# A chunked RWKV-7 recurrence with a squared-ReLU FFN on one core: products written in turn to two partition halves, x made by halves, sums and words taken earlier

## The chip, the cores and the metric

The kernel runs on one core of a Trainium2 chip. Its engines each work through their own list of instructions in order: TensorE (PE in the profile; PEld is its weight load) multiplies matrices and writes PSUM, VectorE (DVE) and ScalarE (ACT) read PSUM and work elementwise, GpSimd (POOL) works elementwise on SBUF, SyncE (SP) issues DMAs. ACT and POOL issue DMAs too. The metric is the device time of one execution in microseconds (us), lower is better.

## The reference

Four sequences, 8 heads, 768 steps, head size 40. Each head keeps a 40 x 40 state; then a feed-forward layer of width 2048 works on the result.

```python
for t in range(S):
    y[:, :, t] = np.einsum('bhd,bhde->bhe', rt, state)
    Sa = np.einsum('bhde,bhe->bhd', state, at)
    state_decay = state * wt[:, :, None, :] - np.einsum('bhd,bhe->bhde', Sa, bt)
    state = state_decay + np.einsum('bhd,bhe->bhde', vt, kt)
...
x = attn_out.transpose(0, 2, 1, 3).reshape(B * S, H * D)      # 3072 x 320
h = np.maximum(x @ w_in, 0.0)
return h * h @ w_out
```

All inputs and outputs are float32 for the chip's program.

## The kernel before

The 768 steps are cut into 6 chunks of 128, which gives 24 chunks (sequence by sequence within a chunk number), and `order` counts them 0 to 23. Within a chunk the recurrence becomes matrix products. Let a, b, k, r be scaled by running decays (`up`, `down`). Then

- `early` makes, for each head, the products of b and a (`products`), from which come N, the coupling of the chunk's first 64 rows to its last 64, and two triangular 64 x 64 blocks whose inverses are needed. Five ACT copies take them from PSUM into the tile `N` (lines 399 to 403); DMAs carry them to DRAM: `kept_q` or `kept_d` for the blocks, `kept_m` and `kept_n` for the rest.
- The triangular blocks are inverted on POOL by substitution (`solving`, lines 469 to 489), many heads and chunks side by side. A *unit* is what POOL inverts at once: 1 to 4 chunks. Units 0 to 8 invert quarter blocks of 32; units 9 and 10, chunks 16 to 19 and 20 to 23, invert blocks of 64 in 63 steps. `take` fetches a unit's words into `half_n`, `solving` stores the result in `kept_t`, and `inverses` loads it from there as T for one chunk.
- `chain` does what only follows from the state. x = a·state + A·v, for 128 rows, is gathered in one PSUM bank (`x_`). Its first half is copied by ACT into `x_first`, multiplied by T (here T0), copied back, multiplied by N and added to the second half of x in the bank; the second half is copied to `x_second` and multiplied by T (here T1). The result, negated, is `minus_x`. Heads go in pairs: 4 products of 128 x 64 by 128 x 80 each for T0, N and T1. In the trace each float32 product is two PE instructions.
- `closing` ends a chunk: the state grows by k·v and b·minus_x (both products go into one bank, `grown`; the last chunk of a sequence has none), and the outputs `y_` gather RV·k and RX·b. RV and RX are masked products. ACT copies the last decay into `end`.
- `Ffn` works on pairs of chunks (*groups*, 0 to 11): `thirds` and `whole` are x·w_in, ReLU and square are on ACT (lines 777 and 784), and `make_quarter` is the product with w_out. From group 5 on, that product is done by seven block products for eight (Strassen's way), the *pieces* P1 to P7 (`make_piece`), whose sums DVE makes. In groups 5 to 10, P6, P5 and P3 write three parts of one PSUM bank. For the last group each has a bank of its own.

Up to chunk 7 the order of the work is a list of words written by hand (the *opening*; `f` is a product of the identity, `fill_in`, whose result nobody reads: the word's number is 128-column blocks). From chunk 7 on a fixed order repeats, one *slot* per chunk (`sorted_slot`): a slot does the end of its chunk's chain, prepares the next chunk, makes in slots 7 to 13 one or two early parts of later chunks, and does FFN work between. At its end stand the squares, then the next chunk's x (slots 7 to 22, 16 of them), and then the steps of `closing` alternate with T0, N and T1 of the next chunk's chain. Two pieces come at the end of each slot and two at the start of the next. After slot 23 follows the tail, with FFN work alone.

[...] The framework sets the semaphores between engines.

Of the kernel before, what the change touches and what calls it, by code (L numbers as in the profile page):

```python
# [17 lines left out]
def kernel(  # L18
# [341 lines left out]
    def early(i, g=None, apart=False):  # L360
# [36 lines left out]

        even, odd = products(bT, aT[:, :, :C])
        nc.scalar.copy(t_[:HC, :, :NP], even[:HC].rearrange("s h (f t) -> s f h t", f=2))  # L399
        nc.scalar.copy(t_[HC:, 1, NP:], even[HC:, :, HC:])  # L400
        nc.scalar.copy(t_[HC:, 1, :NP], odd[:HC, :, :HC])
        nc.scalar.copy(t_[:HC, 0, NP:], odd[HC:, :, HC:])
        nc.scalar.copy(t_[:HC, 1, NP:], odd[:HC, :, HC:])
        moved = []
# [13 lines left out]
        if g is None:  # L418
            moved.append((kept_n[i].rearrange("b s q t -> s b q t"), t_[:HC, 1].rearrange("s (b q) t -> s b q t", b=2), nc.sync))
        if opened:  # L420
# [207 lines left out]
    halves = (slice(0, HC), slice(HC, C))  # L628
    by_parity = lambda t_: t_.rearrange("t (q e) d -> t e q d", e=2)

    x_first, x_second = (single(name, [128, NP, 2, D]) for name in ("x_first", "x_second"))
    for t_ in (x_first, x_second):
        nc.gpsimd.memset(t_, 0.0)

    def chain(i, g):
        bb, c = order[i]
        st = states.tiles[bb]
        first, second_ = halves
        k_, b_, v_, rT = (g[x] for x in ("k", "b", "v", "rT"))

        x_ = psum(ps_c)[:, :DM].rearrange("t (h d) -> t h d", h=H)
        if c > 0:
            for q in range(NP):
                for f in range(2):
                    mm(x_[halves[f], 2 * q:2 * q + 2], g["aT"][:, q, f * HC:(f + 1) * HC], st[:, q, :, :D], q == 0)
        for h in range(H):
            for f in range(2):
                mm(x_[halves[f], h], g["A"][h % 2][:, h // 2, f * HC:(f + 1) * HC], v_[:, h, :D], c == 0 and h == 0)
        for e in range(2):
            nc.scalar.copy(x_first[halves[e], :, e], by_parity(x_)[first, e])  # L650
# [12 lines left out]
        for e in range(2):
            nc.scalar.copy(x_first[halves[e], :, e], xs[:, :, e])  # L664
        nc.scalar.copy(xn[first, :, :D], xs.rearrange("t q e d -> t (q e) d"))
        yield
        for q in range(NP):
            mm(x_[second_, 2 * q:2 * q + 2], N[:, q], both(x_first[:, q]), False)
        for e in range(2):
            nc.scalar.copy(x_second[halves[1 - e], :, e], by_parity(x_)[second_, e])  # L670
# [21 lines left out]
    def closing(i, g, y_, rx, xn):  # L692
# [46 lines left out]
    class Ffn:  # L739
# [72 lines left out]
        def make_piece(self, g, at):  # L812
# [43 lines left out]
            if at == 4:  # L856
                self.sixth = ps[0]
            if at == (4 if last else 6):
                plus(hi1, self.sixth, hi1)
                plus(hi0, self.sixth, hi0)  # L860
                less(lo1, hi1, lo1)
            if at == 5:
                self.fifth = ps[1]
            if at == (5 if last else 6):
                plus(hi1, self.fifth, hi1)
                plus(hi0, self.fifth, hi0)
            if at == 6:
                plus(hi0, ps[2], hi0)
            for n in {5: (1,), 6: (0,)}.get(at, ()) if last else (1, 0) if at == 6 else ():
# [216 lines left out]
    def sorted_slot(i, g, ch):  # L1086
# [76 lines left out]
    for i in range(LAID, len(order)):  # L1163
# [44 lines left out]
```

## Time and profile before

| | |
|---|---|
| three runs | 950.64, 959.54, 959.63 us (median 959.54) |
| the profiled execution | 953.11 us, of which the span from first to last instruction is 951.4 |
| busy | PE 885.5 us, POOL 458.3, DVE 446.3, ACT 344.7 |
| T, N and T1 instructions | 192 each (24 chunks x 4 products x 2) |
| opening, slots 7 to 22, rest | to about 330 us, to about 859 us, to 951 us |

In the rows of the timeline the first number is the start in us from the span's start, the second the length of a row of like instructions. What stands in brackets is idle time of the engine before it and what ended it. A row such as `128*64 128x80` has 128 rows of contraction, 64 output rows, and 80 columns that are streamed.

### The profile page before, as it was taken

The numbers are of one execution on the slowest core, as the hardware profiler recorded it, in microseconds if no ns is written. First come the engines' busy times: TensorE is split into PE (matmuls) and PEld (weight loads), VectorE is DVE, ScalarE is ACT, GpSimd is POOL, SyncE is SP. The second block draws the span as 40 slices with busy tenths as digits, with TensorE's granted clock in tenths as the row PEclk, the third lists the DMA queues.
The fourth block names the chain that finished last, engine by engine and source line by source line (L and its number), as shares of the span: only waits on it lengthen the run. The fifth ranks groups of instructions, "written<-read, shape, count | busy, mean of one in ns | idle before, by whom it ended". The sixth has DMA issues, their size and how long they took to land.

```text
span 951.4 us, 22372 instructions
## 1 busy us (share of the span) xinstructions
PE 885.5 (93%) x9004; PEld 741.0 (78%) x9004; DVE 446.3 (47%) x1127; ACT 344.7 (36%) x797; POOL 458.3 (48%) x869
## 2 busy tenths in 40 slices
PE   6668978879899999989999999999999999999998
PEld 5446656758687877868888878898988988888897
DVE  4827757886843343454432553363534523233022
ACT  3032334534633335524434424423333233332311
POOL 4557447083007686770189998599997000000000
PEclk9768989589899999999999999999999999999999
DMA  9759869947766578697874545544414444130000
GB/s 110 125 125 154 185 125 189 223 101 141 166 104 150 96 136 171 136 159 128 162 142 91 104 70 102 142 73 86 79 29 110 75 83 78 23 63 2 21 14 14
DMA packets 257137, 102.04 MB, mean 107 GB/s; under 512 B 235211, under 2 KB 246859, under 8 KB 256011
## 3 DMA queue, kind: packets, MB, share of 16 engines
q1 hardware_dynamic: 248613, 83.00, 48.7%
q0 software_dynamic: 3664, 15.79, 6.7%
q10 hardware_dynamic: 4757, 1.83, 0.9%
q8 instruction: 71, 1.16, 0.6%
q14 instruction: 32, 0.25, 0.1%
HBM read 67.82 MB, written 30.79 MB: 104 GB/s over the span
## 4 chain that ended last, share of the span: by engine, by line
PE 75%; DVE 8%; ACT 6%; DMA 5%; SPq 3%; issue 2%; ACTq 0%; POOL 0%; DVEq 0%; POOLq 0%
PE ps_f L87 37%; PE ps_w L87 18%; PE ps_c L87 10%; PE ps_w L331 5%; DMA in_ab<-in_b_dram 2%; PE ps_f L264 2%; DMA dec<-kept_e 1%; ACT x_first L664 1%; PE ps_c L600 1%; PE ps_c L676 1%; DMA in_r<-in_r_dram 1%; ACT hid L784 1%; DVE half_t L480 1%; DVE half_t L482 1%; SPq L421 1%
## 5 line engine op out<-in xcount | busy, mean ns | idle before, releaser
L480 POOL TENSOR_TENSOR half_p<-half_n,half_t 128x126 f32<-128x126 f32 (+43 forms) x374 | 196.4, 525 | 68.8 <-DMA half_n<-kept_q 24.2
L482 POOL TENSOR_TENSOR half_t<-half_t,half_p 128x126 f32<-128x126 f32 (+43 forms) x374 | 212.9, 569 | 29.3
L87 PE MATMUL ps_f<-tokens,w_in 128*128 128x256 f32 x672 | 157.9, 389 | 0.0
L87 PE MATMUL ps_f<-w_out,hid 128*128 128x160 f32 (+1 forms) x736 | 151.8, 359 | 0.0
L87 PEld LDWEIGHTS ps_f<-tokens,w_in 128*128 128x128 f32 x672 | 126.6, 193 | 24.2 <-issue 7.3
L87 PEld LDWEIGHTS ps_f<-w_out,hid 128*128 128x128 f32 x736 | 116.1, 190 | 22.3
L777 ACT ACTIVATE hid<-ps_f 128x512 f32<-128x512 f32 x84 | 49.2, 596 | 121.2 <-PE ps_f L87 120.4
L453 POOL DMA_DIRECT2D half_n<-kept_q x20 | 10.4, 526 | 94.7 <-DMA kept_m<-N 33.2
L708 DVE TENSOR_TENSOR state<-ps_w,state 40x160 f32<-40x160 f32 x40 | 12.8, 320 | 90.4 <-PE ps_w L87 90.1
L784 ACT ACTIVATE hid<-hid 128x512 f32<-128x512 f32 x96 | 54.6, 625 | 0.1
L347 DVE TENSOR_TENSOR RX<-ps_w,upper 128x512 f32<-128x512 f32 x48 | 30.9, 684 | 46.6 <-PE ps_w L87 46.6
L372 DVE TENSOR_TENSOR_SCAN decay<-ps_w,ones 128x64 f32<-128x64 f32 x88 | 23.8, 270 | 60.4 <-PE ps_w L331 60.4
L87 PE MATMUL ps_f<-tokens,w_third 64*128 64x256 f32 x336 | 49.9, 391 | 2.3 <-DVE o L843 2.2
L722 DVE TENSOR_TENSOR tokens<-ps_c,dec 128x512 f32<-128x512 f32 x24 | 16.6, 692 | 71.3 <-PE ps_c L87 69.9
L399 ACT COPY N<-ps_w 64x512 f32<-64x512 f32 x24 | 13.9, 579 | 99.6 <-PE ps_w L87 71.6
L264 PE MATMUL ps_f<-ident 128*128 128x512 f32 (+3 forms) x108 | 49.5, 592 | 0.0
L347 DVE TENSOR_TENSOR RV<-ps_w,upper 128x512 f32<-128x512 f32 x48 | 30.9, 685 | 18.5 <-PE ps_w L87 18.2
L87 PEld LDWEIGHTS ps_f<-tokens,w_third 64*128 64x128 f32 x336 | 31.9, 189 | 8.2 <-DVE o L843 3.8
L331 PE MATMUL ps_w<-ident,in_ab 128*128 128x128 f32 x184 | 27.6, 295 | 11.0 <-DVE RV L347 8.7
L550 DVE TENSOR_TENSOR kvT<-ps_w,dec 128x512 f32<-128x512 f32 x24 | 16.5, 686 | 43.8 <-PE ps_w L331 37.8
L87 PE MATMUL ps_w<-rT,kvT 40*128 40x128 f32 x384 | 29.5, 295 | 6.1 <-ACT kvT L563 6.1
L562 ACT COPY rT<-ps_w 128x512 f32<-128x512 f32 x24 | 14.0, 584 | 57.7 <-PE ps_w L331 57.7
(179 smaller groups left out, 1639.7 us busy)
## 6 DMA issues: line engine op xcount, KB each, us to landing
dec<-kept_e SPq DMA_DIRECT2D x22, 633.8 KB
kept_e<-decay SPq DMA_DIRECT2D x19, 633.8 KB
in_w<-in_w_dram SPq DMA_DIRECT2D x24, 160.0 KB
in_b<-in_b_dram SPq DMA_DIRECT2D x24, 160.0 KB
in_ab<-in_a_dram SPq DMA_DIRECT2D x24, 160.0 KB
in_r<-in_r_dram SPq DMA_DIRECT2D x24, 160.0 KB
in_v<-in_v_dram SPq DMA_DIRECT2D x24, 160.0 KB
half_n<-kept_q POOLq DMA_DIRECT2D x14, 256.0 KB, 4.8
```

Of the source, the lines that this page charges most:

```text
L87: nc.tensor.matmul(o, l_, r_, start=start, stop=True, skip_group_check=True)
L264: nc.tensor.matmul(fill_bank[:, :n * 128], ident, ident.unsqueeze(1).to_broadcast([128, n, 128]), start=True, stop=True, skip_group_check= ...
L331: nc.tensor.transpose(p_[:, q * 128:(q + 1) * 128], pair(x_, q), ident)
L347: nc.vector.tensor_tensor(t_, p_, over4(upper), Alu.mult)
L372: nc.vector.tensor_tensor_scan(up[:, q, MID + 1:C + 1], wT[:, q, MID:], ones, 1.0, Alu.mult, Alu.mult)
L480: eng.tensor_tensor(p_, part[:, at:at + m_].unsqueeze(1).to_broadcast([128, n, m_]), t3[:, :n, s:s + 1].to_broadcast([128, n, m_]), Alu.mult)
L482: eng.tensor_tensor(t3[:, :n, s + 1:], t3[:, :n, s + 1:], p_, Alu.subtract)
L550: nc.vector.tensor_tensor(kT, kT_, down[:, :, 1:C + 1], Alu.mult)
L562: nc.scalar.copy(g["rT"], p_)
L722: nc.vector.tensor_tensor(t_, y_, g["up"][:, :, :C], Alu.mult)
L777: nc.scalar.activation(h_, p_.rearrange("p f t -> p (f t)"), Act.Relu)
L784: nc.scalar.activation(h_, h_, Act.Square)
```

## The change

1. `chain`: T0, N and T1 take the head pairs in the order 0, 2, 1, 3, and write pairs 0 and 1 to partitions 0 to 63, pairs 2 and 3 to 64 to 127. For this the places of the heads in N and T differ: `early` fills `N` by ten ACT copies, eight of 64 x 128 and two of 64 x 256, where it took one of 64 x 512 and four of 64 x 256. `kept_n` is stored by two DMAs with runs of 512 B, where it was one with runs of 1 KB.
2. x is made by halves of its rows: `begin_x(0)`, two copies, `begin_x(1)`. One tile `apart_x` serves for `x_first` and `x_second`. The copies into `minus_x` are two of 64 x 160 for one of 64 x 320, and those of the first half come after N.
3. In the slot the chain's step comes first in each round (T0 ahead of the growth of the state), and the first of four RX products of `closing` moves ahead of T1.
4. `make_piece`: the sums with P6 and P5 follow these pieces in every group, where groups 5 to 10 made them after P3.
5. Unit 9 is inverted up to step 48, then the first 2048 words of unit 10 are fetched, then the rest of unit 9 is done.

```diff
-        even, odd = products(bT, aT[:, :, :C])
-        nc.scalar.copy(t_[:HC, :, :NP], even[:HC].rearrange("s h (f t) -> s f h t", f=2))
-        nc.scalar.copy(t_[HC:, 1, NP:], even[HC:, :, HC:])
-        nc.scalar.copy(t_[HC:, 1, :NP], odd[:HC, :, :HC])
-        nc.scalar.copy(t_[:HC, 0, NP:], odd[HC:, :, HC:])
-        nc.scalar.copy(t_[:HC, 1, NP:], odd[:HC, :, HC:])
+        for e, p_ in enumerate(products(bT, aT[:, :, :C])):
+            for group in range(2):
+                own_, qs = slice(group * HC, (group + 1) * HC), slice(2 * group, 2 * group + 2)
+                nc.scalar.copy(t_[own_, group, e:NP:2], p_[:HC, qs, :HC])
+                nc.scalar.copy(t_[own_, group, NP + e::2], p_[HC:, qs, HC:])
+            nc.scalar.copy(t_[:HC, 1, e::2], p_[:HC, :, HC:])
...
+            for e in range(2):
+                moved.append((kept_n[i][e].rearrange("s (w j) t -> s w (j t)", w=2), between[:, :, e].rearrange("s w j t -> s w (j t)"), nc.sync))
...
+    in_turn_ = (0, 2, 1, 3)
...
+        def begin_x(f):
+            cols = slice(f * HC, (f + 1) * HC)
+            if c > 0:
+                for q in in_turn_:
+                    mm(x_[halves[q // 2], f, 2 * q % NP:2 * q % NP + 2], g["aT"][:, q, cols], st[:, q, :, :D], f == 0 and q % 2 == 0)
+            for h in range(NP):
+                for e in range(2):
+                    mm(x_[halves[e], f, h], g["A"][h % 2][:, 2 * e + h // 2, cols], v_[:, e * NP + h, :D], c == 0 and f == 0 and h == 0)
...
+        begin_x(0)
+        to_apart(lambda e: x_[halves[e], 0])
+        begin_x(1)
...
-        def times_t(half, x):
-            xs = psum(ps_w)[:, :DM].rearrange("t (q c) -> t q c", q=NP)
-            for q in range(NP):
-                mm(xs[halves[half], q], T[:, half * NP + q], both(x[:, q]), q == 0)
+        def times_t(half):
+            xs = psum(ps_w)[:, :DM // 2].rearrange("t (j c) -> t j c", j=2)
+            for q in in_turn_:
+                mm(xs[halves[q // 2], q % 2], T[:, half * NP + q], both(q), q % 2 == 0)
...
+        for n in in_turn_:
+            mm(x_[halves[n // 2], 1].rearrange("t (b j) d -> t b j d", b=2)[:, :, n % 2], N[:, n], both(n), False)
+        to_xn(0, xs)
+        to_apart(lambda e: x_[halves[e], 1])
...
+        to_y(rx, b_, 0)
+        yield
+        for q in range(1, NP):
             to_y(rx, b_, q)
...
-            if at == (4 if last else 6):
+            if at == 4:
                 plus(hi1, self.sixth, hi1)
                 plus(hi0, self.sixth, hi0)
                 less(lo1, hi1, lo1)
...
-            if at == (5 if last else 6):
+            if at == 5:
                 plus(hi1, self.fifth, hi1)
                 plus(hi0, self.fifth, hi0)
...
             for _ in range(3):
+                next(n["chain"])
                 next(close)
-                next(n["chain"])
...
-            take(unit, own)
-            solve(unit)
+            words = [slice(None)] if under_way is None else [slice(0, EARLIER), slice(EARLIER, None)]
+            take(unit, own, words[0])
+            if under_way is not None:
+                run(under_way)
+                take(unit, own, words[1])
+            under_way = solving(unit, (48,) if FINE <= unit < len(units) - 1 else ())
+            next(under_way, None)
```

What it does to PE's list at the end of slot 14, where chunk 15's x stands (`state_137,dec_131` and `in_v_112,A` are x's two parts, `in_v_114` and `minus_x_132` the growth of chunk 14's state). Before:

```order
L87 MATMUL ps_c<-state_137,dec_131 64x80 [waits Activation_49]
L87 MATMUL ps_c<-state_137,dec_131 64x80 x7
...
L87 MATMUL ps_c<-in_v_112,A 64x40 x13
L87 MATMUL ps_w<-in_v_114,in_k_106 40x40 x8
L87 MATMUL ps_w<-minus_x_132,in_b_86 40x40 x8
L87 MATMUL ps_c<-RV,in_k_106 64x128 x2
L87 MATMUL ps_w<-x_first,T 64x80 [waits Activation_49]
...
L87 MATMUL ps_c<-RV,in_k_106 64x128 x6
L87 MATMUL ps_c<-x_first,N_7059 64x80 [waits DMAHW6_49,Activation_49]
...
L87 MATMUL ps_c<-RX,in_b_86 64x128 x8
L87 MATMUL ps_w<-x_second,T 64x80 [waits Activation_49]
```

And with the change, the same place:

```order
L87 MATMUL ps_c<-in_v_112,A 64x40 x5
L87 MATMUL ps_c<-state_137,dec_131 64x80 [waits Activation_49]
...
L87 MATMUL ps_c<-in_v_112,A 64x40 x8
L87 MATMUL ps_w<-apart_x,T 64x80 x4
L87 MATMUL ps_w<-in_v_114,in_k_106 40x40 x8
L87 MATMUL ps_w<-minus_x_132,in_b_86 40x40 x8
L87 MATMUL ps_c<-RV,in_k_106 64x128 x2
L87 MATMUL ps_c<-apart_x,N_7183 64x2x40 [waits DMAHW3_49,Activation_49]
...
L87 MATMUL ps_c<-RV,in_k_106 64x128 x6
L87 MATMUL ps_c<-RX,in_b_86 64x128 x2
L87 MATMUL ps_w<-apart_x,T 64x80 [waits Activation_49]
...
L87 MATMUL ps_c<-RX,in_b_86 64x128 x6
```

x stands in two parts, and the second begins with a wait for ACT; T0 has none of its own, and the growth of the state comes behind it. (The list counts a float32 product once, the trace twice.)

The second place is on PE at the end of slot 19, where P6 (`decay_127,hid`) and P5 of group 7 stand, and at the start of slot 20, where P3 stands behind the transposes of r and v. Before:

```order
L87 MATMUL ps_f<-decay_127,hid 128x160 [waits PE_49]
L87 MATMUL ps_f<-decay_127,hid 128x160 x7
L87 MATMUL ps_f<-w_out,hid 128x160 x8
L331 MATMUL ps_w<-ident,in_r_110 128x128 [waits DMAHW3_49]
...
L87 MATMUL ps_f<-w_out,hid 128x160 x8
```

And with the change:

```order
L87 MATMUL ps_f<-decay_127,hid 128x160 [waits PE_49]
L87 MATMUL ps_f<-decay_127,hid 128x160 x7
L87 MATMUL ps_f<-w_out,hid 128x160 [waits DVE_49]
L87 MATMUL ps_f<-w_out,hid 128x160 x7
L331 MATMUL ps_w<-ident,in_r_110 128x128 [waits DMAHW0_49]
...
L87 MATMUL ps_f<-w_out,hid 128x160 [waits DVE_49]
```

P5's first product waits for DVE, where it waited for nothing, and so does P3's.

The third place is on POOL, between unit 9 and unit 10 (`half_t` and `half_p` are the substitution's steps, `kept_t_233` unit 9's result). Before:

```order
L482 TENSOR_TENSOR half_t<-half_t,half_p 128x32 [waits Pool_49]
L489 DMA kept_t_233<-half_t 128x2048 [waits Pool_49]
L453 DMA half_n<-kept_d_223 64x3072 [waits DMAHW4_49,DMAHW5_49,DMAHW3_49,DMAHW6_49,DMAHW2_49,DMAHW7_49,DMAHW1_49,DMAHW0_49]
L453 DMA half_n<-kept_d_223 64x3072
L469 MEMSET half_t 128x2048 [waits DMASW1_49]
```

And with the change:

```order
L485 TENSOR_TENSOR half_t<-half_t,half_p 128x24x16 [waits Pool_49]
L456 DMA half_n<-kept_d_223 64x2048 [waits DMAHW3_49,DMAHW5_49,DMAHW2_49,DMAHW7_49,DMAHW1_49,DMAHW0_49]
L456 DMA half_n<-kept_d_223 64x2048
L483 TENSOR_TENSOR half_p<-half_n,half_t 128x375 [waits Pool_49]
...
L492 DMA kept_t_233<-half_t 128x2048 [waits Pool_49]
L456 DMA half_n<-kept_d_223 64x1024 [waits DMAHW4_49,DMAHW3_49,DMAHW6_49,DMAHW2_49,DMAHW0_49]
```

The fetch of the first words, with its wait for the stores of chunks 20 to 23, moved from behind unit 9's result to ahead of its last 15 steps.

More of the change, by code (lines that the diff above doesn't have):

```diff
@@ L418, in early @@
         if g is None:
-            moved.append((kept_n[i].rearrange("b s q t -> s b q t"), t_[:HC, 1].rearrange("s (b q) t -> s b q t", b=2), nc.sync))
+            between = t_[:HC, 1].rearrange("s (w b j) t -> s w b j t", w=2, b=2)
+            for e in range(2):
+                moved.append((kept_n[i][e].rearrange("s (w j) t -> s w (j t)", w=2), between[:, :, e].rearrange("s w j t -> s w (j t)"), nc.sync))
         if opened:
@@ L427, in early @@
             for e in range(2):
-                nc.scalar.copy(g["N"][e * HC:(e + 1) * HC], t_[:HC, 1, e * NP:(e + 1) * NP])
+                nc.scalar.copy(g["N"][e * HC:(e + 1) * HC].rearrange("s (w j) t -> s w j t", w=2),
+                               t_[:HC, 1].rearrange("s (w b j) t -> s w b j t", w=2, b=2)[:, :, e])
             g["joins"] = spare("joins", i)
@@ L628 @@
     halves = (slice(0, HC), slice(HC, C))
[L629 to L633, printed above, removed]
+    apart_x = single("apart_x", [128, NP, 2, D])
+    nc.gpsimd.memset(apart_x, 0.0)
+    in_turn_ = (0, 2, 1, 3)
     def chain(i, g):
@@ L637, in chain, with to_apart @@
         st = states.tiles[bb]
-        first, second_ = halves
         k_, b_, v_, rT = (g[x] for x in ("k", "b", "v", "rT"))
-        x_ = psum(ps_c)[:, :DM].rearrange("t (h d) -> t h d", h=H)
-        if c > 0:
-            for q in range(NP):
[L644 to L650, printed above, removed]
+        x_ = psum(ps_c)[:, :DM].rearrange("t (f h d) -> t f h d", f=2, d=D)
+        def begin_x(f):
[6 more added lines that the diff above has]
+                    mm(x_[halves[e], f, h], g["A"][h % 2][:, 2 * e + h // 2, cols], v_[:, e * NP + h, :D], c == 0 and f == 0 and h == 0)
+        def to_apart(of):
+            for e in range(2):
+                nc.scalar.copy(apart_x[halves[e], :, e], of(e))
+        begin_x(0)
+        to_apart(lambda e: x_[halves[e], 0])
+        begin_x(1)
         yield
@@ L653, in chain, with to_xn @@
         xn = minus_x.next()
-        both = lambda t_: t_.rearrange("p e d -> p (e d)")
-        def times_t(half, x):
-            xs = psum(ps_w)[:, :DM].rearrange("t (q c) -> t q c", q=NP)
-            for q in range(NP):
-                mm(xs[halves[half], q], T[:, half * NP + q], both(x[:, q]), q == 0)
-            return xs[halves[half]].rearrange("t q (e d) -> t q e d", e=2)
-        xs = times_t(0, x_first)
+        both = lambda q: apart_x[:, q].rearrange("p e d -> p (e d)")
+        def times_t(half):
+            xs = psum(ps_w)[:, :DM // 2].rearrange("t (j c) -> t j c", j=2)
+            for q in in_turn_:
+                mm(xs[halves[q // 2], q % 2], T[:, half * NP + q], both(q), q % 2 == 0)
+            return xs.rearrange("t j (w d) -> t w j d", w=2)
+        def to_xn(half, xs):
+            for e in range(2):
+                to = xn[halves[half], :, :D].rearrange("t (w b j) d -> t w b j d", w=2, b=2)[:, :, e]
+                nc.scalar.copy(to, xs[halves[e]])
+        xs = times_t(0)
         for e in range(2):
-            nc.scalar.copy(x_first[halves[e], :, e], xs[:, :, e])
-        nc.scalar.copy(xn[first, :, :D], xs.rearrange("t q e d -> t (q e) d"))
+            nc.scalar.copy(apart_x[halves[e], :, e].rearrange("t (w j) d -> t w j d", w=2), xs[halves[e]])
         yield
[L667 to L670, printed above, removed]
+        for n in in_turn_:
+            mm(x_[halves[n // 2], 1].rearrange("t (b j) d -> t b j d", b=2)[:, :, n % 2], N[:, n], both(n), False)
+        to_xn(0, xs)
+        to_apart(lambda e: x_[halves[e], 1])
         yield
-        nc.scalar.copy(xn[second_, :, :D], times_t(1, x_second).rearrange("t q e d -> t (q e) d"))
+        to_xn(1, times_t(1))
         yield
@@ L714, in closing @@
             to_y(g["RV"], k_, q)
+        to_y(rx, b_, 0)
         yield
-        for q in range(NP):
+        for q in range(1, NP):
             to_y(rx, b_, q)
@@ L868, in make_piece @@
                 plus(hi0, ps[2], hi0)
-            for n in {5: (1,), 6: (0,)}.get(at, ()) if last else (1, 0) if at == 6 else ():
+            for n in {5: (1,), 6: (0,)}.get(at, ()):
                 bb, c = order[g * GB + n]
@@ L1059 @@
     done = set(range(14))
-    unit = len(solves)
+    unit, under_way = len(solves), None
     def fetch_next(i, *names):
@@ L1171 @@
             flush()
-            take(unit, own)
-            solve(unit)
+            words = [slice(None)] if under_way is None else [slice(0, EARLIER), slice(EARLIER, None)]
[5 more added lines that the diff above has]
+            next(under_way, None)
+            if unit < FINE or unit == len(units) - 1:
+                run(under_way)
+                under_way = None
             unit += 1
```

## The prediction

> **What bounds the kernel now.** I read the page first: how much of the span each engine works.
>
> ```profile
> span 951.4 us, 22372 instructions
> PE 885.5 (93%) x9004; PEld 741.0 (78%) x9004; DVE 446.3 (47%) x1127; ACT 344.7 (36%) x797; POOL 458.3 (48%) x869
> ```
>
> TensorE (PE) is busy 93% of the span, the next engine 48%. The view by stretches says where it is not busy (columns: stretch, its length, then each engine's busy us and instructions, the clock, the DMA share).
>
> ```profile
> 618.00:648.50 30.50, 30.42 (x330) 27.75 (x329) 15.61 (x22) 9.91 (x23) 28.30 (x29) 1.00 0.33 58
> 648.50:678.40 29.90, 29.01 (x314) 25.94 (x313) 10.44 (x22) 9.46 (x21) 27.94 (x26) 1.00 0.41 74
> ```
>
> A slot (one chunk of the steady part) leaves PE 0.08 us idle of 30.5; the next leaves 0.89. A "busy" PE is not yet a PE that could do nothing else: a matmul's row holds its latency. So I looked at the end of a slot in the timeline of PE and ACT, where the changed products stand (start, length, engine, line, tiles, shape, count).
>
> ```profile
> 611.96 0.78 PE L87 MATMUL ps_c<-state,dec 128*64 128x80 f32 x16
> 612.56 1.08 PE L87 MATMUL ps_c<-in_v,A 128*64 128x40 f32 x32
> 613.47 0.48 PE L87 MATMUL ps_w<-in_v,in_k 128*40 128x40 f32 x16
> 614.08 0.42 PE L87 MATMUL ps_c<-RV,in_k 128*64 128x128 f32 x4
> 614.34 0.70 PE L87 MATMUL ps_w<-x_first,T 128*64 128x80 f32 x7
> 615.84 0.56 PE L87 MATMUL ps_c<-x_first,N 128*64 128x80 f32 x5
> 616.45 1.04 PE L87 MATMUL ps_c<-RX,in_b 128*64 128x128 f32 x14
> 617.32 0.74 PE L87 MATMUL ps_w<-x_second,T 128*64 128x80 f32 x8
> 617.99 0.81 PE L87 MATMUL ps_f<-in_ab,hid 128*128 128x160 f32 x4
> ...
> 612.56 1.14 ACT L784 ACTIVATE hid<-hid 128x512 f32<-128x512 f32 x2
> 613.69 0.59 ACT L650 COPY x_first<-ps_c 64x160 f32<-64x160 f32 x2
> 614.31 0.20 ACT L710 COPY end<-dec 128x4 f32<-128x4 f32 x1
> 615.20 0.59 ACT L664 COPY x_first<-ps_w 64x160 f32<-64x160 f32 x2 [0.69 <-PE ps_w L87]
> 616.65 0.59 ACT L670 COPY x_second<-ps_c 64x160 f32<-64x160 f32 x2 [0.41 <-PE ps_c L87]
> ```
>
> The stretch of 6.03 us (611.96 to 617.99) is a relay: x on PE, copies on ACT, T0 on PE, copies, N, copies, T1. Each hand-over takes 0.05 to 0.06 us: T0 starts 0.06 after L650's copies end (614.28), N 0.05 after L664's (615.79). PE's other rows only fill the gaps. And the copies of x start when two things end together: x (612.56+1.08 = 613.64) and ACT's squares, L784 (612.56+1.14 = 613.70).
>
> **The products in turn: what they save.** Start to start, T1's 8 instructions take 617.99-617.32 = 0.67. The state products have the same shape (128x64, 80 columns), but write to the two halves in turn: 16 in 612.56-611.96 = 0.60, or 8 in 0.30. T, N and T1 now do so too: 0.37 less each. I take 0.30; if their order gains nothing it is 0.67. Were PE's issue the bound, that were 3 x 0.37 = 1.1 per chunk.
>
> **x by halves: a wait that the text of the diff doesn't show.** The new order is first half of x, its copies, second half, T0; the second half is to run while ACT copies the first. In the list of PE's instructions its first one waits for ACT, and T0, which reads what ACT copied, waits for ACT no more. So the second half waits for those very copies: it writes the bank that they read. Queued behind the waiting instruction on PE are the rest of the slot's end and the next slot; nothing else can be issued. [...]
>
> With the rows' numbers, us from 611.96. Half of x is (613.47-611.96)/2 = 0.76, its result 0.17 later: 0.93. The copies can't start before ACT's squares end: 1.74, to 2.33. Second half 2.38 to 3.14. T0 to 3.44, result 3.61. Copies 3.66 to 4.25. PE meanwhile: the state's growth (614.08-613.47 = 0.61) and the first RV (0.26), to 4.31. N to 4.61. ACT has the end copy (0.20) and the pair of minus_x copies that now stands ahead, 0.59, so N's copies run 5.04 to 5.63. PE's other 12 RV (614.34-614.08 = 0.26 per four) and first 4 RX ((617.32-616.45)/14 = 0.062 each) last from 4.61 to about 5.6. T1 5.68 to 5.98, and 12 RX after it, 0.75: 6.73, against 6.03 now. That is +0.70. In the last three slots, which have no growth and no end copy, the same sum gives +0.60. In the first three, ACT's squares end earlier, as in this row of one of them:
>
> ```profile
> 401.16 0.59 ACT L650 COPY x_first<-ps_c 64x160 f32<-64x160 f32 x2 [0.28 <-PE ps_c L87]
> ```
>
> ACT idles 0.28 before the copies, so +0.4. Sixteen slots begin a chain (10 x 0.70 + 3 x 0.60 + 3 x 0.4 = 10.0; I take 9.6, 0.6 each, for copies that overlap by some hundredths). Ends: were there no wait, T0 would start at 2.38 as now, the same steps would end the relay at 5.93, and sixteen times -0.1 is -1.6; it is +24 if the new order of T, N and T1 gains nothing (1.5 each).
>
> **Sums of a piece.** Now six sums follow the last piece of a group, and PE waits for its bank:
>
> ```profile
> 650.76 2.34 PE L87 MATMUL ps_f<-w_out,hid 128*128 128x160 f32 x16
> 656.19 0.33 DVE L843 TENSOR_TENSOR in_w<-ps_f,in_w 128x160 f32<-128x160 f32 x1 [7.47 <-PE ps_f L87]
> 656.43 0.32 DVE L843 TENSOR_TENSOR o<-ps_f,o 128x160 f32<-128x160 f32 x1
> 658.47 1.13 PE L87 MATMUL ps_f<-tokens,w_third 64*128 64x256 f32 x6 [0.80 <-DVE o L843]
> PE ps_f L87 <- DVE o L843: 2.2, 4, 0.8
> ```
>
> The last row (the view of waits) says 2.2 us in four waits. These go: one sum of 0.32 is left after the last piece, and products of 1.1 us stand before the bank is wanted. But P5 writes the bank that P6's sums read, and its first matmul, free now, waits for DVE in the new list: 0.04 to start, two sums to 656.75 (0.56), 0.06 to PE: 0.67. P5 of group 5 is the row at 650.76; ahead of it is P6, and nothing between. Four groups in slots, two in the tail, and P3 behind P5 in the last of these: 7 x 0.67 = 4.7. Net +2.5 (-2.2 to +4.7).
>
> **The opening: copies of N, stores, and x.** N takes ten copies for five:
>
> ```profile
> L399 ACT COPY N<-ps_w 64x512 f32<-64x512 f32 x24 | 13.9, 579 | 99.6 <-PE ps_w L87 71.6 <-issue 18.6 <-DMA in_ab<-in_b_dram 6.5
> L650 ACT COPY x_first<-ps_c 64x160 f32<-64x160 f32 x48 | 13.7, 285 | 28.0 <-PE ps_c L87 27.5
> L402 ACT COPY N<-ps_w 64x256 f32<-64x256 f32 x24 | 8.9, 369 | 0.3
> ```
>
> 0.58 + 4 x 0.37 = 2.05 becomes 2 x 0.37 + 8 of 64x128. Between 64x160 (0.285) and 64x512 (0.579) an element costs 0.83 ns, so 64x128 is 0.26: 2.82, +0.78 a chunk. In a slot ACT idles past that (9.9 busy of 30.5). The opening makes N for 14 chunks; I take four of these as lying on its path (an estimate, between none and all): +3. The store of N for later chunks becomes two, one issue more on SP or ACT per chunk (0.69 in the row below), for two of them: +1.4. Then the wait of x, which is worst where ACT is behind:
>
> ```profile
> 120.36 1.13 PE L87 MATMUL ps_c<-in_v,A 128*64 128x40 f32 x32
> 121.42 6.71 PE L264 MATMUL ps_f<-ident 128*128 128x512 f32 x16
> 134.46 1.06 PE L87 MATMUL ps_w<-spares 32*32 32x32 f32 x32 [3.31 <-DVE spares L522]
> ...
> 125.64 0.69 ACTq L421 DMA_DIRECT2D kept_n<-N x1
> 127.62 0.56 ACT L650 COPY x_first<-ps_c 64x160 f32<-64x160 f32 x2
> ```
>
> x of chunk 2 ends at 121.5, its copies only at 128.2, because ACT has N's copies and seven issues first. PE fills that time with 16 fill products. With the change PE stands until 128.2+1.4 = 129.6, then the other half 0.6, the fill 6.7, and transposes and fill to 134.46 that took 6.5 but 3.3 of idle: spares at 140.1 instead of 134.46, up to +5.7. What DMA and VectorE are late by anyway swallows some: I take half, +3. Against it, T, N and T1 of eight chains, 24 x 0.37 = 8.9 at most; on the path about half, -4. Opening: +3.4, from -6 to +11.
>
> **Hidden.** Unit 10's words come early, in the midst of unit 9's solve on POOL.
>
> ```profile
> 577.27 1.84 SPq L110 DMA_DIRECT2D kept_d<-N x4
> 594.95 0.60 POOL L489 DMA_DIRECT2D kept_t<-half_t x1 [0.30 <-POOL half_t L482]
> 608.94 0.29 POOL L480 TENSOR_TENSOR half_p<-half_n,half_t 128x63 f32<-128x63 f32 x1 [6.49 <-DMA half_n<-kept_d]
> 625.66 1.83 SPq L509 DMA_DIRECT2D T<-kept_t x2
> 733.45 0.60 POOL L489 DMA_DIRECT2D kept_t<-half_t x1 [0.30 <-POOL half_t L482]
> 746.79 1.39 SPq L509 DMA_DIRECT2D T<-kept_t x2
> ```
>
> POOL would wait for the words' store (issued 577 to 579) with fifteen steps of unit 9 queued behind; unit 9's result moves from 595 to about 608, before its reader at 625.7, and unit 10's from 733 to about 740, before 746.8. Cover: 13 us, then 7. Cost none; gone, each us late is one lost.
>
> **Sum.** The profiled execution took 953.11 (span 951.4 and 1.7 around it). 953.1 + 9.6 + 2.5 + 3.4 = 968.6. The three runs' median, 959.54, lies 6.4 above it, so I add half of that: **972**.
>
> **Rivals.** *Faster: PE's issue is the bound.* If the second half of x starts before ACT's squares end (the point that decides) and PE finds work for every gap, the stretch is PE's work and shrinks by 1.1: 16 x 1.1 = 17.8; with -4 and +2.5 the time is 953.1 - 19.3 + 3.2 = 937. For it: 0.08 us of idle in a slot. Against it: the hand-overs of 0.05 us and ACT's row. 0.13. *No change:* ACT comes to the copies as soon as the first half is ready (0.98 for 1.74), the stretch is then 6.73 - 0.76 = 5.97, sixteen times -0.06, and the opening swallows its losses: 953.1 - 1.0 + 2.5 + 3.2 = 958. For it: squares that end just when x does may end sooner when x does. Against it: they wait for FFN products that the change leaves alone. 0.24. *Slower still:* the opening carries all (+11), or the products in turn gain half: 953.1 + 9.6 + 2.5 + 11 + 7 = 983. 0.13. My forecast, 0.50, with its own range 962 to 982.
>
> The range leaves out the faster rival and a little of the last: 952 to 985. Within 1% is about what a measurement of this kernel can't tell from no change (its three runs span 9 us). Slower: 0.13, most of 0.50, and 0.03 of the second: 0.60. Same 0.27, faster 0.13.
>
> **What would show it.** In the new profile: in each slot the state products in two rows, PE idle some 1.4 us between them with ACT's copy of x as releaser; rows of T, N and T1 near 0.55 instead of 0.75; P5 behind a wait of 0.67 on DVE, and no wait of the third-products on DVE; N's copies 2.8 us a chunk. Wrong would be a second half of x that starts with ACT still copying, or slots that get shorter.

## The result, and the profile after

The changed kernel took 993.81 us (median of four, 992.27 to 995.10), the kernel before 959.59 in the same comparison: ratio 1.039 (95% interval 1.032 to 1.046). It is slower, as forecast, but by 34 us and not by 12: 972 was the forecast, 985 its upper end. The page of the profiled execution (995.1 us):

```profile
span 993.4 us, 22626 instructions
PE 883.9 (89%) x9004; PEld 736.1 (74%) x9004; DVE 446.4 (45%) x1127; ACT 366.4 (37%) x965; POOL 454.8 (46%) x871
```

PE has as many instructions as before and is busy 883.9 us, 1.6 less; the span is 42.0 longer. So PE is idle 43.6 us more; that it is also slower while it counts as busy turned out to be part of it. The same end of a slot as in the prediction, chunk 17's, in the timeline of PE and of ACT:

```profile
705.98 0.50 PE L87 MATMUL ps_c<-state,dec 128*64 128x80 f32 x8
706.30 0.61 PE L87 MATMUL ps_c<-in_v,A 128*64 128x40 f32 x16
708.25 0.50 PE L87 MATMUL ps_c<-state,dec 128*64 128x80 f32 x8 [1.33 <-ACT apart_x L656]
708.58 0.61 PE L87 MATMUL ps_c<-in_v,A 128*64 128x40 f32 x16
709.02 0.48 PE L87 MATMUL ps_w<-apart_x,T 128*64 128x80 f32 x8
709.32 0.47 PE L87 MATMUL ps_w<-in_v,in_k 128*40 128x40 f32 x16
...
710.24 0.50 PE L87 MATMUL ps_c<-apart_x,N 128*64 128x80 f32 x8
...
711.71 0.50 PE L87 MATMUL ps_w<-apart_x,T 128*64 128x80 f32 x8
...
707.62 0.58 ACT L656 COPY apart_x<-ps_c 64x160 f32<-64x160 f32 x2
```

The second half of x starts 0.05 us after the copies of the first (707.62 + 0.58 = 708.20). From x's start T0 comes at 3.04 (forecast 3.14), N at 4.26 (4.31), T1 at 5.73 (5.68), and a row of eight takes 0.30 (709.32 - 709.02) for 0.67. The waits of PE over the whole span (sum, times, longest):

```profile
PE ps_c L87 <- ACT apart_x L656: 42.0, 24, 6.8
...
PE ps_w L331 <- DMA in_r<-in_r_dram: 6.5, 1, 6.5
...
PE ps_f L87 <- DVE o L859: 4.5, 7, 0.7
```

The wait inside x comes in all 24 chunks (that its sum equals the span's difference is chance: other terms come and go beside it). Where the 42 us lie is seen when the span is cut at the starts of A·v's row in chunks 7, 15 and 23. I use this table for every run; each row is one profiled execution. The changed kernel, profiled a second time, differs from its row by at most 1.4 us in a column.

| us | to chunk 7 | chunks 7 to 15 | 15 to 23 | rest | span |
|---|---|---|---|---|---|
| before | 330.4 | 282.1 | 240.8 | 98.1 | 951.4 |
| changed | 343.9 | 301.0 | 246.6 | 101.9 | 993.4 |
| difference | +13.5 | +18.9 | +5.8 | +3.8 | +42.0 |
| forecast | +3.4 | +4.2 | +5.3 | +2.6 | +15.5 |

(The forecast's 0.6 a slot falls on chunks 8 to 14, 15 to 22, and 23; of the sums 0.5 on the slots and 2.0 on the rest.) The third column came out as forecast. The first two hold the error. The second column's chunks differ from the third's in one thing that the timeline shows at once, the length of PE's rows. Chunk 11's x:

```profile
501.16 0.50 PE L87 MATMUL ps_c<-state,dec 128*64 128x80 f32 x8 [2.19 <-ACT apart_x L656]
501.48 0.74 PE L87 MATMUL ps_c<-in_v,A 128*64 128x40 f32 x16
502.02 0.78 PE L87 MATMUL ps_w<-apart_x,T 128*64 128x80 f32 x8
502.59 0.75 PE L87 MATMUL ps_w<-in_v,in_k 128*40 128x40 f32 x16
503.13 0.74 PE L87 MATMUL ps_w<-minus_x,in_b 128*40 128x40 f32 x16
```

T0's eight take 0.57 here, the growth 1.07 (503.66 is the next row's start), where chunk 17 needs 0.30 and 0.61. The view by stretches says why (length, then busy us and instructions of PE, PEld, DVE, ACT and POOL, the granted clock, DMA share, GB/s):

```profile
498.40:501.81 3.41, 1.22 (x41) 1.10 (x38) 0.00 (x0) 2.68 (x7) 2.86 (x8) 1.00 0.18 48
501.81:505.22 3.41, 3.41 (x68) 3.41 (x66) 0.64 (x2) 1.59 (x6) 3.02 (x6) 0.50 0.77 183
505.22:508.64 3.42, 3.42 (x41) 2.77 (x38) 0.69 (x1) 0.89 (x4) 3.03 (x6) 1.00 0.34 71
...
676.00:679.41 3.41, 2.08 (x66) 1.96 (x68) 0.00 (x0) 2.09 (x5) 3.17 (x4) 1.00 0.00 0
679.41:682.82 3.41, 3.31 (x83) 2.76 (x76) 0.65 (x2) 2.49 (x9) 3.17 (x4) 1.00 0.03 7
```

After 3.41 us in which PE worked 1.22, the clock is granted at half for the next 3.41. After 3.41 with 2.08 of work (chunk 16) it stays full. Before, no such stretch came between 330 us and the last products; now eight do, 27 us in all.

### The profile page after: what moved, and what is told of

The parts are those of the page before. It is cut to its first block, busy times and chain, and to the rows that moved or that the text cites. A ratio compares the mean times of both kernels' runs of the same rounds, so it can differ in the third digit from the quotient of the medians.

```text
span 993.4 us, 22626 instructions
## 1 busy us (share of the span) xinstructions
PE 883.9 (89%) x9004; PEld 736.1 (74%) x9004; DVE 446.4 (45%) x1127; ACT 366.4 (37%) x965; POOL 454.8 (46%) x871
## 4 chain that ended last, share of the span: by engine, by line
PE 67%; ACT 13%; DVE 7%; DMA 4%; issue 3%; SPq 1%; ACTq 0%; DVEq 0%
PE ps_f L87 32%; PE ps_w L87 17%; PE ps_c L87 9%; PE ps_w L331 5%; ACT hid L800 3%; PE ps_f L264 3%; ACT apart_x L656 2%; ACT N L402 2%; DMA in_r<-in_r_dram 1%; ACT N L401 1%; ACT hid L793 1%; DMA dec<-kept_e 1%; PE ps_c L691 1%; ACT T L544 1%; ACT N L403 1%
## 5 line engine op out<-in xcount | busy, mean ns | idle before, releaser
L485 POOL TENSOR_TENSOR half_t<-half_t,half_p 128x126 f32<-128x126 f32 (+43 forms) x374 | 209.6, 560 | 29.3
L87 PE MATMUL ps_f<-w_out,hid 128*128 128x160 f32 (+1 forms) x736 | 154.2, 362 | 4.5 <-DVE o L859 4.5
L401 ACT COPY N<-ps_w 64x128 f32<-64x128 f32 x96 | 24.7, 258 | 104.2 <-PE ps_w L87 90.2
L87 PE MATMUL ps_c<-state,dec 128*64 128x80 f32 x320 | 19.9, 245 | 31.3 <-ACT apart_x L656 31.3
L87 PE MATMUL ps_f<-tokens,w_third 64*128 64x256 f32 x336 | 46.7, 388 | 0.1
L87 PEld LDWEIGHTS ps_c<-state,dec 128*64 128x64 f32 x320 | 13.4, 136 | 39.9 <-ACT apart_x L656 33.7
L87 PE MATMUL ps_c<-in_v,A 128*64 128x40 f32 x768 | 31.5, 231 | 10.9 <-ACT apart_x L656 10.7
L656 ACT COPY apart_x<-ps_c 64x160 f32<-64x160 f32 x96 | 27.3, 284 | 32.7 <-PE ps_c L87 30.9
```

The source lines that it names most:

```text
L87: nc.tensor.matmul(o, l_, r_, start=start, stop=True, skip_group_check=True)
L401: nc.scalar.copy(t_[own_, group, e:NP:2], p_[:HC, qs, :HC])
L485: eng.tensor_tensor(t3[:, :n, s + 1:], t3[:, :n, s + 1:], p_, Alu.subtract)
L656: nc.scalar.copy(apart_x[halves[e], :, e], of(e))
```

## The experiments

The theory after these readings: (a) the wait inside x costs PE's idle time in every chunk; (b) where it idles long, in slots whose ACT also makes N, half clock follows; (c) SP's second store of N puts a load behind POOL's in the opening; (d) the ten copies themselves and the sums cost little. The rivals were the prediction's own small terms, and, for the slots, that the products or the copies cost it. Each ratio is to runs of the kernel before in the same comparison; columns are compared with the table above. Thirteen runs of the kernel before in one comparison lie between 944 and 958 us, so a difference of a few us in the medians says little by itself.

### x whole again

```diff
         begin_x(0)
-        to_apart(lambda e: x_[halves[e], 0])
         begin_x(1)
+        to_apart(lambda e: x_[halves[e], 0])
```

> The changed kernel with x made whole again: both halves first, then the two copies of the first half, so that PE has no wait inside x. All else as changed. Theory (the wait inside x costs twice, once as a longer relay and once because the long idle of PE in slots 7 to 14 is followed by about 3.4 us at half clock; N's ten copies and the stores cost the rest): of the 42.0 us between the two spans, the 5.1 of chunk 2's x in the opening go, 14 of the 18.9 of slots 7 to 14 and all 5.8 of slots 15 to 22; 994 - 25 = about 969 us (965 to 975), no window of half clock in the slots. Rival (products that write in turn are what costs, or the copies of N alone): the time stays within 5 us of 994.

967.0 us, ratio 1.019 (1.016 to 1.021). Columns 335.5, 287.3, 239.9, 101.2: against the changed kernel 8.4, 13.7, 6.7 and 0.7 less. From chunk 8's x to the last products there is no half clock; one stretch stays in slot 7 (at 357.2), where none was expected. So 29 of the 42 us between the spans hang on the wait that the halves of x bring. By the medians it is 27, by the ratios to the kernel before 19 to 22.

### The wait kept, PE's idle time filled

```diff
         to_apart(lambda e: x_[halves[e], 0])
+        if i > LAID:
+            cover = psum(ps_w)
+            for n in (4, 2):
+                nc.tensor.matmul(cover[:, :n * 128], ident, ident.unsqueeze(1).to_broadcast([128, n, 128]),
+                                 start=True, stop=True, skip_group_check=True)
         begin_x(1)
```

> The changed kernel, with products of the identity (six blocks of 128 columns, 1.3 us on PE, result never read) between the halves of x in the slots, where PE waits at least 1.33 us: the wait stays, PE's idle time in it goes or shrinks to 0.4 to 0.9 us. Theory (idle PE closes the clock): the half-clock windows that begin in the slots at 348, 382, 423, 502, 539, 577, 614 and 833 us go, but for the one at 348, and each is worth 1 to 1.5 us: 7 to 10 us, 994 to about 985. Rival (PE waits for ACT anyway, so the clock costs nothing, or fill only adds work): 994 or up to 1 us a slot more, 1000.

984.6 us (981.4 to 994.5), ratio 1.038 (1.033 to 1.044); 983.4 the profiled span, 10 under the changed kernel's. The ratio alone can't tell it from the changed kernel; the trace can. Columns 341.3, 294.3, 245.9, 102.0. Chunk 12's x:

```profile
530.34 1.56 PE L663 MATMUL ps_w<-ident 128*128 128x512 f32 x4
532.55 0.50 PE L87 MATMUL ps_c<-state,dec 128*64 128x80 f32 x8 [0.66 <-ACT apart_x L656]
532.88 0.61 PE L87 MATMUL ps_c<-in_v,A 128*64 128x40 f32 x16
533.32 0.48 PE L87 MATMUL ps_w<-apart_x,T 128*64 128x80 f32 x8
533.62 0.47 PE L87 MATMUL ps_w<-in_v,in_k 128*40 128x40 f32 x16
```

The second half waits for the same copies, yet T0's eight take 0.30 again, and the growth 0.61. All the half-clock windows of the slots are gone but the one at the last x of the opening, which had no fill. Columns two and three are 7.4 us shorter (6.7 and 0.7): the price of the half clock alone, by work that nobody reads. Chunk by chunk it is sharper: the seven slots that had half clock behind them (after the x of chunks 8, 9, 11 to 14 and 21) are 1.1 to 1.4 us shorter, the others between nothing and 0.2 longer. (The 2.6 of the first column is not the fill's, which stands in the slots alone.) The wait's own price is what the run with x whole gains beyond that, 7.0 and 6.0.

### N by ten copies, in the kernel before

```diff
-        nc.scalar.copy(t_[:HC, :, :NP], even[:HC].rearrange("s h (f t) -> s f h t", f=2))
-        nc.scalar.copy(t_[HC:, 1, NP:], even[HC:, :, HC:])
...
+        for f in range(2):
+            nc.scalar.copy(t_[:HC, f, :NP], even[:HC, :, f * HC:(f + 1) * HC])
+        for n in (0, 2):
+            nc.scalar.copy(t_[HC:, 1, NP + n:NP + n + 2], even[HC:, n:n + 2, HC:])
...
```

> The kernel before, with N filled by ten ACT copies (two of 64x256, eight of 64x128) to the same places, for five; its stores as before. Theory (in slots 7 to 13 the copies are not hidden: ACT's squares, and with them the copies of x, come 0.7 us later): 0.7 in each of the seven slots that make N, with the opening +3: +5 to +8, about 967 us. Rival (the prediction's words, hidden in a slot): +3, 962.5.

962.8 us, ratio 1.014 (1.011 to 1.017): more than either expected. Columns 331.9, 291.2, 239.9, 98.0. The opening loses 1.5. Of the 9.1 in the second column 9.3 come at one place, between chunks 14 and 15. (The others cancel: 1.8 in four slots, and -2.0 at a wait in slot 9 that is missing here.) It is a load; the wait of PE, SP's issue and POOL's:

```profile
PE ps_w L87 <- DMA spares<-kept_m: 4.2, 1, 4.2
...
596.68 1.47 SPq L502 DMA_DIRECT2D spares<-kept_m  x2
...
594.97 1.03 POOL L455 DMA_DIRECT2D half_n<-kept_d  x2
```

SP's load for chunk 15 is issued 1.7 us behind POOL's fetch of unit 10's words; before, it was issued 2.7 ahead of it (592.99 and 595.70) and nobody waited. The 4.2 us of waiting are not all: PE is idle 3.37 of the 3.41 us from 604.24 on, and the clock stands at half for the next 10.24, half of which makes the other 5.1 of the 9.3. So the direct price of the copies is 1.5 us in the opening and some 2 in the slots, and the rest is a late load that this kernel has and the changed one, where SP loads these rows at 587.57 and POOL fetches at 610.57, has not.

### N stored by two DMAs, in the kernel before

```diff
-            moved.append((kept_n[i].rearrange("b s q t -> s b q t"), t_[:HC, 1].rearrange("s (b q) t -> s b q t", b=2), nc.sync))
+            for n in (0, 2):
+                moved.append((kept_n[i].rearrange("b s q t -> s b q t")[:, :, n:n + 2].rearrange("s b q t -> s b (q t)"),
+                              t_[:HC, 1].rearrange("s (b q) t -> s b q t", b=2)[:, :, n:n + 2].rearrange("s b q t -> s b (q t)"), nc.sync))
```

> The kernel before, with the coupling rows of N stored by two DMAs in runs of 512 B where it was one in runs of 1 KB; copies as before. Theory (SP's two extra issues per chunk in the opening put the loads of r and of b, a behind POOL's loads, and r of chunk 1 lands 6.5 us later): +5 to +9, about 966 us. Rival (the prediction's term, the issues alone): +1.4, 961; a third, the loads are late only together with the longer copies: 960.

970.7 us, ratio 1.024 (1.020 to 1.028). Columns 338.4, 288.1, 239.7, 98.2: 8.0 in the opening, of which 6.1 lie between the x of chunks 0 and 1, and 6.0 in the second column: 7.4 from the same late load of chunk 15 as above, again with half clock behind it (6.83 us), less 2.0 at the wait in slot 9. The opening's place, in this kernel (PE, SP, POOL), and then SP and POOL of the kernel before:

```profile
80.79 1.09 PE L331 MATMUL ps_w<-ident,in_r 128*128 128x128 f32 x4 [5.92 <-DMA in_r<-in_r_dram]
...
66.31 0.60 SPq L146 DMA_DIRECT2D in_r<-in_r_dram  x1
...
65.63 1.06 POOL L455 DMA_DIRECT2D half_n<-kept_q  x2 [8.71 <-DMA kept_q<-N]
```

```profile
66.87 0.67 SPq L146 DMA_DIRECT2D in_r<-in_r_dram  x1
...
66.81 1.05 POOL L453 DMA_DIRECT2D half_n<-kept_q  x2 [8.23 <-DMA kept_q<-N]
```

The load of r for chunk 1 was issued 0.06 us after POOL's fetch, and is now issued 0.68 after it. That costs 5.9 us of waiting.

### One store of 2 KB runs, in the changed kernel

```diff
-            for e in range(2):
-                moved.append((kept_n[i][e].rearrange("s (w j) t -> s w (j t)", w=2), between[:, :, e].rearrange("s w j t -> s w (j t)"), nc.sync))
+            moved.append((kept_n[i], t_[:HC, 1], nc.sync))
...
-            queue.dma_start(out=g["N"], in_=kept_n[i].rearrange("b s q t -> (b s) q t"))
+            for e in range(2):
+                queue.dma_start(out=g["N"][e * HC:(e + 1) * HC].rearrange("s (w j) t -> s w (j t)", w=2),
+                                in_=kept_n[i].rearrange("s (w b j) t -> s w b (j t)", w=2, b=2)[:, :, e])
```

> The changed kernel with one edit: the coupling rows of N stored by one DMA in runs of 2 KB and loaded by two, so SP and ACT issue one store for two. Theory (what makes r of chunk 1 late is that SP's second store puts its load behind POOL's fetch): the wait for r falls from 6.5 to under 1, the opening is 6 to 8 us shorter, ratio about 1.031 where the changed kernel has 1.039. Rival (the ten copies alone make r late enough): no gain in the opening, ratio 1.039.

983.4 us, ratio 1.033 (1.027 to 1.040). Columns 336.0, 301.1, 245.0, 103.3: 7.9 less in the opening (8.6 between the x of chunks 0 and 1), and the wait for r is not in the list of waits any more. SP issues the load at 66.56, POOL the fetch at 66.62. The slots are as in the changed kernel.

### The changed kernel on the same chip

> The changed kernel again, for the same chip as the two others: ratio 1.032 to 1.046 as measured before, with half-clock windows in the slots in which PE idles 1.7 us or more within one window of 3.41 us.

993.9 us, ratio 1.042 (1.034 to 1.050). Columns 342.9, 301.0, 245.6, 103.3, and half clock after the x of chunks 8, 9, 11, 12, 13 and 14 again, not after that of chunk 10. So the store is worth 10.6 us between the medians of the two (7 of them in the profile's opening).

### The sums of P6 and P5, in the kernel before

```diff
-            if at == (4 if last else 6):
+            if at == 4:
                 plus(hi1, self.sixth, hi1)
...
-            if at == (5 if last else 6):
+            if at == 5:
                 plus(hi1, self.fifth, hi1)
```

> The kernel before, with the sums of pieces P6 and P5 made right after these pieces in groups 5 to 10 too. All else as before. Theory (the prediction's term): +2.5 us, from seven waits of PE for DVE of 0.6 to 0.7 (4.5 in all) for the 2.2 of now: ratio 1.0026. Rival (the changed kernel's last part, after the last x, is 3.9 us longer, and that is all the sums): +4 to +5, ratio 1.005. A third: slower by more than 6, if late pieces push the next slot's loads behind POOL's.

Ratio 1.003 (0.999 to 1.007). The wait is 4.5 us in seven places, as in the changed kernel, and the rest column is 2.7 longer, the third 1.3 shorter (0.9 and 1.1 shorter with the old sums too, in the two runs on N in the kernel before). The measured time agrees with the term, and with no change as well.

### The state's growth ahead of T0

```diff
             for _ in range(3):
-                next(n["chain"])
                 next(close)
+                next(n["chain"])
```

with x whole.

> The changed kernel with x whole and, in the slot, the step of closing first in each round, as in the kernel before: the state's growth stands ahead of T0 and fills PE's idle 0.92 us between x and T0 (1.6 in slots 10 to 13). Else as changed. Theory (PE's time in a slot is what counts as soon as no wait stands in x, and part 3 of the change moved 0.6 us of work out of the one gap that the slot has): 0.5 to 0.6 us less in each of 13 slots with growth than with x whole alone: 967 - 7 = 960, ratio about 1.011. Rival (the relay through ACT bounds the slot, so where the growth stands is nothing): 967, ratio 1.0186.

957.2 us, ratio 1.008 (1.005 to 1.012). Columns 334.4, 285.8, 233.4, 100.5. PE in chunk 17's x:

```profile
679.25 0.61 PE L87 MATMUL ps_c<-in_v,A 128*64 128x40 f32 x16
679.68 0.48 PE L87 MATMUL ps_w<-in_v,in_k 128*40 128x40 f32 x16
679.99 0.48 PE L87 MATMUL ps_w<-minus_x,in_b 128*40 128x40 f32 x16
680.30 0.41 PE L87 MATMUL ps_c<-RV,in_k 128*64 128x128 f32 x4
680.56 0.50 PE L87 MATMUL ps_w<-apart_x,T 128*64 128x80 f32 x8
```

Growth and RV fill the time between x and T0. In the third column that is 6.5 us over eight chunks, 0.8 each (0.5 to 0.6 expected). With x whole alone, T, N and T1 had become 3 x 0.37 = 1.1 shorter per chunk and the slot hardly at all (-0.9 in eight): part 3 of the change had taken the work out of the gap that the new products left. In the second column one place hides the gain: in slot 9 PE waits 5.1 us for VectorE, 6.83 at half clock follow, and the slot takes 5.4 longer, where the seven others are 6.9 shorter together.

### The parts that help, together

```diff
-        to_xn(0, xs)
         to_apart(lambda e: x_[halves[e], 1])
+        to_xn(0, xs)
```

with x whole, growth first, sums as before, and one store of N.

> The kernel of the run with growth first, and three more edits: the second copies of x (for T1) ahead of minus_x's copies of the first half on ACT; the sums of P6 and P5 as in the kernel before; the coupling rows of N stored by one DMA in runs of 2 KB and loaded by two. N still takes ten copies, T, N and T1 write in turn. Theory: T1 starts 0.4 us sooner in each slot, but PE has then no more work to wait with, 0.2 to 0.4 us a slot (5); the sums give 2.5, the store 5 to 8 in the opening (r of chunk 1 lands in time again): ratio 1.011 - 0.014 = 0.997 (0.990 to 1.004). Rival (the ten copies are what makes r late, and the opening stays as it is): 1.004 or more.

942.5 us, ratio 0.991 (0.988 to 0.995): faster than both kernels. Columns 327.8, 278.0, 234.2, 97.8. The opening is 2.6 shorter than before in spite of the ten copies, eight slots of the third column 6.6. The moved copies bring nothing: T1 starts 4.88 us after x here and in the run before. In chunks 11 to 14 T0 comes at 3.09 to 3.13 and not at 2.38, for ACT is behind with N, and the second column gains less: of its 4.1 us 2.7 are a wait in slot 9 that the kernel before had in its profile (2.65) and this one has not.

### Four of N's copies on VectorE

```diff
-                nc.scalar.copy(t_[own_, group, NP + e::2], p_[HC:, qs, HC:])
+                nc.vector.tensor_copy(t_[own_, group, NP + e::2], p_[HC:, qs, HC:])
```

> The kernel of the run before this one in the call (all edits), with four of N's ten copies (those of the last 64 rows of products) on VectorE instead of ACT. Theory: ACT's part falls from 2.8 to 1.8 us a chunk, so in slots 10 to 13 the copies of x come 0.7 us sooner, when the squares end, as in slots 14 on: 3 to 5 us less than without, ratio about 0.993. Rival (VectorE gets late in the opening, where PE waits for it): the opening longer by 2 or more, ratio 1.00.

963.8 us, ratio 1.012 (1.005 to 1.019), the rival. Columns 346.5, 284.0, 236.2, 97.7: against the fastest kernel the opening is 18.7 longer (7 of them ahead of chunk 0's x; the clock stands at half for 130 us of it, 78 in the fastest kernel), and the slots gain nothing. The copies don't run side by side: up to 340 us VectorE's wait 41.3 us for ACT's copies of N, ACT's 13.6 for VectorE's.

### Two pairs to one half, then two to the other

```diff
-            for q in in_turn_:
+            for q in range(NP):
                 mm(xs[halves[q // 2], q % 2], T[:, half * NP + q], both(q), q % 2 == 0)
...
-        for n in in_turn_:
+        for n in range(NP):
```

in the fastest kernel.

> The kernel with all edits that was faster than before (ratio 0.991), with T0, N and T1 in the order of pairs 0, 1, 2, 3 for 0, 2, 1, 3: the same products and places, but the first two write one half of the partitions and then the last two the other. Theory (a product that follows one on the same half waits for it, 0.09 us a time: 0.53 less 0.26 over three successions): a row's eight instructions take 0.44 from first to last start for 0.26; in slots 15 to 22, where PE's own work bounds the end of the slot, 3 x 0.18 = 0.5 a slot, 4 us in all, nothing in slots 8 to 14 where PE waits for ACT: ratio 0.996. Rival (only the layout, two pairs to a half, counts): rows stay at 0.26, ratio 0.991.

945.1 us, ratio 0.994 (0.991 to 0.997). T0's row and the one that follows:

```profile
642.33 0.50 PE L87 MATMUL ps_w<-apart_x,T 128*64 128x80 f32 x8
642.65 0.83 PE L87 MATMUL ps_c<-RV,in_k 128*64 128x128 f32 x12
```

0.32 for eight, as in turn. The third column is 234.9 for 234.2; of the 5.4 us between the spans 3.5 arise in slot 9, where PE waits 2.4 for VectorE once and 3.41 at half clock follow. So it is the spread over both halves that shortens the row, and the order within the row is worth 0.1 us a chunk at most. My explanation "in turn" was too narrow, the duration right.

## Why the prediction was wrong

Direction and mechanism were right: the relay is bound by ACT's copies, the second half of x waits for those of the first, and the shorter T, N and T1 are not gained. That second half has other addresses than the first and waits 24 times of 24 (42.0 us). (x lies in one bank and is also one tile of the program: no run here tells which of the two the wait is for.) Step by step:

- **The relay (+9.6).** In slots 14 to 19 of the changed kernel it is what was worked out, T1 at 5.73 for 5.68 (6.57 in slot 20, behind half clock); the third column gives +5.8 with the sums in it. Right.
- **"In a slot ACT idles past that": failed.** I read ACT's idle time from a slot that makes no N. In slots 10 to 13 ACT has no gap between N's copies and x's. The same stretch before and after:

```profile
505.87 0.58 ACT L399 COPY N<-ps_w 64x512 f32<-64x512 f32 x1 [3.90 <-PE ps_w L87]
...
511.13 1.16 ACT L784 ACTIVATE hid<-hid 128x512 f32<-128x512 f32 x2
512.17 0.60 ACT L650 COPY x_first<-ps_c 64x160 f32<-64x160 f32 x2
```

```profile
530.79 0.26 ACT L401 COPY N<-ps_w 64x128 f32<-64x128 f32 x1 [3.90 <-PE ps_w L87]
...
536.77 1.16 ACT L800 ACTIVATE hid<-hid 128x512 f32<-128x512 f32 x2
537.80 0.59 ACT L656 COPY apart_x<-ps_c 64x160 f32<-64x160 f32 x2
```

  6.30 us from N's first copy to x's, then 7.01: the 0.71 arrive whole at x, and PE's idle time in x becomes 2.1 to 2.2 for 1.33. I had costed N's copies against the busy share of the wrong slot.
- **A term that was missing: the clock.** A wait of PE was priced as the time it lasts. Behind the waits in the x of chunks 8, 9 and 11 to 14, with 1.71 to 2.19 us of PE's idle time in one window of 3.41, half clock followed for 3.41 us: 6.7 us in the second column (the run with the filled wait). With the wait itself (7.0) and what is left with x whole (5.2) that makes its 18.9.
- **"One issue more ... for two of them: +1.4": failed.** I priced the issue, 0.69, and not the loads behind it. The load of r fell 0.6 us behind POOL's fetch and PE waited 6.5: 8.0 us in the opening alone, 7.9 when taken back. The prediction quoted SP's queue for POOL's part and never asked for SP's own next issue.
- **x in the opening: "I take half, +3".** PE stood 6.75 us at chunk 2's x, and chunk 3's x came 5.1 later against before than chunk 2's had, near the upper end, 5.7. With x whole the opening is 8.4 shorter.
- **The copies in the opening (+3)** are 1.5; **the gain of the products there (-4)** is what closes the sum: 1.5 + 8.0 + 8.4 - 13.5 = 4.4, an inference from four profiles and not measured alone. Nor is it exact: the run with the sums alone leaves the opening's instructions as they are, and there too stretches from one x to the next differ from before by -2.9 to +2.4 and cancel.
- **The sums (+2.5): the waits came as worked out** (4.5 in seven places for 4.7); the time, 0.003 of 951 or 2.8, has an interval that reaches zero.
- **POOL's early words, cost none: right.** Unit 9's result is stored at 635.35 in the changed kernel and first loaded at 659.11; PE has no wait for T.

Of the rivals, "slower still" at 983 had the opening carry all, +11, and it came to +13.5, with the late load of r in it, which no rival named; its other half, products that gain half, was false, and what stood in its place was the clock. (The 983 also leaves out the 3.2 that the forecast and the other two rivals have for the median; with it the rival stands at 986, above the range.) The range's upper end was taken from the terms that I had, and the one that I had not thought of lay outside it.

## What to carry to other kernels

A wait is priced by what it leaves behind, too: an idle stretch of PE may cost its length once more in clock (4.2 us and 5.1 at chunk 15's late load), and behind an issue that was 0.6 us late a load came some 5 us late. Ask of each queue which load comes next, and what another queue issues at that time. And read "hidden" from the slot in which the operation runs, not from a neighbour that lacks it; when work is moved forward, look what it leaves uncovered, as the growth of the state did here.

## What the runs showed of the hardware

**The clock.** Half clock came in stretches of 3.41 us or multiples of it (3.41 to 20.48 in the profiles before and after), and every change of the clock in each of these two lies on one grid of 3.41 us. In the slots half clock followed PE's idle time within one window of the grid. Two idle times of nearly the same length, 1.76 and 1.75 us, in the x of chunks 9 and 10 (stretches along the grid):

```profile
419.90:423.31 3.41, 1.65 (x61) 1.53 (x59) 0.00 (x0) 1.99 (x6) 2.86 (x8) 1.00 0.46 92
423.31:426.72 3.41, 3.41 (x54) 3.41 (x50) 0.65 (x2) 1.76 (x7) 2.86 (x7) 0.50 0.96 143
457.44:460.86 3.42, 2.89 (x36) 2.37 (x34) 0.00 (x0) 3.38 (x8) 0.00 (x0) 1.00 0.42 86
460.86:464.27 3.41, 2.19 (x73) 2.05 (x75) 0.29 (x1) 1.92 (x8) 0.00 (x0) 1.00 1.35 159
```

The first lies in one window (PE works 1.65 of 3.41), the second is cut by a boundary, and no half clock follows it. After 300 us, over all thirteen traces, every window that began at full clock and had PE idle for 1.69 us or more was followed by half clock (eight in the changed kernel, 1.69 to 2.31); of three with 1.49 to 1.68, two were; below that one, at 1.09, was. So in these slots about half a window of idle time was enough. In the opening it was looser: full clock followed windows with 1.77 to 1.97 us of idle time (four, between 75 and 136 us; 1.77 at 75 us in the changed kernel), half clock some with less (1.06 at 150 us in the kernel before), down to 0.38, so something besides PE's idle time counts too.

**Loads behind another queue's fetch.** In the thirteen traces r of chunk 1 was issued by SP either within 0.07 us of POOL's fetch (seven kernels; PE waited 1.8 us at most) or 0.61 to 0.68 behind it (six kernels; 5.9 to 6.5). There was nothing between. But the six are the very kernels with two stores of N, so for this load the place behind the fetch and the second store are not told apart. Chunk 15's load speaks for the place: it came late in the run with ten copies too, which has one store. Why so small a difference of the issue makes about 5 us was not settled: the traces don't say to which transfer a packet belongs.

**Products on two halves.** Eight instructions of 128 x 64 by 80 columns took 0.67 on one half of the partitions (T1 in the kernel before) and 0.30 to 0.32 over both, whether in turn (0.30, T0 of chunk 17 in the changed kernel; 0.57 where the clock stood at half, chunk 11) or two pairs at a time (0.32).
